# Attention, two mixture-of-experts layers on one core: VectorE divides the second half of x before it sums the next tile's squares

## The chip, the cores and the metric

The kernel runs on one core of a Trainium2 chip. The metric is the device time of one execution in microseconds (us). Five engines work side by side, each through its own list of instructions in order, and wait for each other by semaphores: PE (TensorE, matrix products), DVE (VectorE), ACT (ScalarE), POOL (GpSimd) and SP (SyncE, which here issues most transfers).

## The reference

Three stages follow each other: attention by random features for 4 batches, 8 heads, 576 positions and 64 dimensions; a mixture of 4 experts in which every expert runs on every token; and a second mixture in which 32 slots gather from all tokens. Only the first stage is touched by the change:

```
def phi(x):                                   # x is q or k, scaled
    proj = np.einsum('bhsd,md->bhsm', x, omega)
    sq = np.sum(x * x, axis=-1, keepdims=True) / 2.0
    h = proj - sq
    h = h - np.max(h, axis=-1, keepdims=True)
    return np.exp(h) / np.sqrt(m)
q_p, k_p = (phi(q_s), phi(k_s))
kv = np.einsum('bhsm,bhsd->bhmd', k_p, v)
z = np.sum(k_p, axis=2)
num = np.einsum('bhsm,bhmd->bhsd', q_p, kv)
den = np.einsum('bhsm,bhm->bhs', q_p, z)[..., None] + 1e-06
return (num / den).astype(np.float32)
```

The result, 2304 tokens of 512 features (`x` below), feeds the first mixture: `h = np.maximum(x @ w1[e], 0.0); out += p[:, e:e + 1] * (h @ w2[e])`.

## The kernel before, in words

The 2304 tokens are 18 tiles of 128. Attention goes through 36 steps, one tile of keys ("k") or of queries ("q") a step. Five k-tiles come first; from step 5 on q and k alternate, up to step 30 (the last k); steps 31 to 35 are q. So the even steps from 6 to 30 are k-steps.

In a step the tiles of several steps are at work at once. What is issued, and in which order on every engine, is a line of two-letter names in the table `orders` (line 310): "k" for a k-step, "q" for a q-step, "qq" for a q behind a q, "" for the drain. `work` (line 321) gives each name its function and its lag: a name with lag 3 works in step i on tile i-3. An engine takes its instructions in the order of these names. No scheduler moves them afterwards.

- `P0`, `P1` (`project`, lines 195 to 197): PE multiplies a tile's first and second four heads with omega into the PSUM tile `pj`, one of three banks in turn.
- `M0`, `M1` (`maximum`, L203), `a0`, `a1` (`bias1`, L208), `b0`, `b1` (`bias2`, L213): DVE's reductions that make the bias `nb` of the exponentials. `a` reads the maximum and the tile's sum of squares.
- `E0`, `E1` (`exps`, L220): ACT makes the features `fe`, four heads in four instructions.
- `S` (`split`, lag -3, L167 on ACT, or on DVE for the last tiles; L170 to L172 on POOL): ACT rounds the tile's numbers into `hi`; POOL computes the rest `lo` (L170), the squares (L171) and a first fold of them (L172).
- `Q` (`squares`, lag -1): DVE sums the next tile's squares (L186), and L187 scales them into the tile `stat`.
- `K0`, `K1` (`accumulate`, L239): PE adds a k-tile's features times v to `kv`.
- `T0`, `T1` (`turn`, lag 1, L253): PE transposes a q-tile's features, ACT copies them (L254).
- `N0`, `N1` (`attend`, lag 3, L263): PE multiplies a q-tile's features with `kv` into `num`, both halves through one PSUM bank.
- `D0`, `D1` (`divide`, lag 3): DVE divides the first and second half (L273, L274, L275) into `x`.
- `X` (`store_x`, lag 4, L284) and `R` (`store_rest`, L290): PE transposes x, ACT and DVE split it for the next stage.

In a k-step `D1` divides the q-tile of three steps before; the q-step behind it transposes that tile's x in `X`. `D1` has work in the k-steps 8 to 30, twelve in all.

Of the kernel before, what the change touches and what calls it, by code (L numbers as in the profile page):

```python
# [17 lines left out]
B, H, S, D = 4, 8, 576, 64  # L18
# [31 lines left out]
def body(ctx: ExitStack, tc: tile.TileContext, ql, kl, vl, om, dp, wl, phi, w2l, out):  # L50
# [244 lines left out]
    def to_dram():  # L295
# [12 lines left out]


    orders = {  # L310
# [1073 lines left out]
```

## Time and profile before

| | |
|---|---|
| time, median of 3 runs | 938.43 us (935.58 to 938.77) |
| profiled execution | 936.1 us, of which the span of the trace is 934.3 us |
| busy share of the span | PE 99%, DVE 80%, ACT 45%, POOL 38% |
| attention stage | the first 150 us of the span, about |
| one k-step and the q-step behind it | 7.70 us |

The span runs from the first to the last instruction of the one profiled execution; the busy shares are means over all stages. The 1.8 us between the profiled time and its span lie outside the trace. PE's share, near 100%, says that it is seldom without work, not that each product runs at its best rate.

### The profile page before, as it was taken

The numbers are of one execution on the slowest core, as the hardware profiler recorded it, in microseconds if no ns is written. First come the engines' busy times: TensorE is split into PE (matmuls) and PEld (weight loads), VectorE is DVE, ScalarE is ACT, GpSimd is POOL, SyncE is SP. The second block draws the span as 40 slices with busy tenths as digits, with TensorE's granted clock in tenths as the row PEclk, the third lists the DMA queues.
The fourth block names the chain that finished last, engine by engine and source line by source line (L and its number), as shares of the span: only waits on it lengthen the run. The fifth ranks groups of instructions, "written<-read, shape, count | busy, mean of one in ns | idle before, by whom it ended". The sixth has DMA issues, their size and how long they took to land.

```text
span 934.3 us, 15959 instructions
## 1 busy us (share of the span) xinstructions
PE 922.3 (99%) x6132; PEld 889.4 (95%) x6132; DVE 750.5 (80%) x1142; ACT 419.7 (45%) x833; POOL 353.4 (38%) x298
## 2 busy tenths in 40 slices
PE   8999999999999999999999999999999999999997
PEld 8999999999999999999999999999999999999734
DVE  7888897999899888888878878887888888878433
ACT  5899875425543434334243333432433434223423
POOL 7978872422443341434053423423241434000100
PEclk9999999999999999999999999999999999999999
DMA  7778768685869675887767666767666776867997
GB/s 259 233 249 299 245 212 267 212 306 175 318 207 343 225 250 197 303 263 264 243 215 254 209 230 214 245 207 258 200 240 203 249 239 201 301 213 276 384 408 309
DMA packets 80510, 236.51 MB, mean 253 GB/s; under 512 B 6636, under 2 KB 34612, under 8 KB 78388
## 3 DMA queue, kind: packets, MB, share of 16 engines
q1 hardware_dynamic: 76260, 222.82, 69.5%
q10 hardware_dynamic: 3744, 9.67, 2.6%
q0 software_dynamic: 432, 3.01, 0.8%
q8 instruction: 48, 0.79, 0.3%
q14 instruction: 26, 0.21, 0.1%
HBM read 211.86 MB, written 23.63 MB: 252 GB/s over the span
## 4 chain that ended last, share of the span: by engine, by line
PE 88%; DVE 7%; ACT 2%; issue 1%; DMA 1%; SPq 0%; POOL 0%; ACTq 0%; DVEq 0%
PE X L809 19%; PE X L633 19%; PE B L633 15%; PE B L809 15%; PE kv L239 3%; PE num L263 3%; PE pj L195 2%; PE so L1233 2%; PE tp L253 2%; PE hq L1205 2%; PE pj L196 2%; PE pj L197 1%; DVE x L831 1%; DMA raw<-kl 1%; PE tpx L284 1%
## 5 line engine op out<-in xcount | busy, mean ns | idle before, releaser
L441 POOL TENSOR_TENSOR Tw<-raww 128x512 f32<-128x512 f32 x30 | 39.8, 1349 | 200.8 <-DMA raww<-wl 200.8
L831 DVE TENSOR_TENSOR x<-X,x 128x768 f32<-128x768 f32 x84 | 79.9, 951 | 40.1 <-PE X L809 39.9
L633 PE MATMUL X<-x,w1h 128*128 128x384 f32 x432 | 110.0, 335 | 0.0
L633 PE MATMUL B<-x,w1h 128*128 128x384 f32 x432 | 109.9, 335 | 0.0
L633 PE MATMUL X<-x,w1x 128*128 128x384 f32 x504 | 94.2, 334 | 0.0
L633 PEld LDWEIGHTS X<-x,w1x 128*128 128x128 f32 x504 | 87.9, 188 | 0.3 <-issue 0.3
L220 ACT ACTIVATE fe<-pj,nb 128x128 f32<-128x128 f32 x288 | 82.8, 390 | 10.1 <-DVE nb L213 9.4
L680 ACT CAST s3h<-X 128x768 fp32r<-128x768 f32 x21 | 16.8, 802 | 143.9 <-DVE X L690 143.9
L633 PEld LDWEIGHTS X<-x,w1h 128*128 128x128 f32 x432 | 77.8, 188 | 0.2 <-ACT u L704 0.2
L633 PEld LDWEIGHTS B<-x,w1h 128*128 128x128 f32 x432 | 77.8, 188 | 0.0
L831 DVE TENSOR_TENSOR x<-B,x 128x768 f32<-128x768 f32 x72 | 68.3, 948 | 6.0 <-PE B L809 5.5
L633 PE MATMUL X<-x,w1l 128*128 128x384 f32 x216 | 72.3, 335 | 0.1
L633 PE MATMUL B<-x,w1l 128*128 128x384 f32 x216 | 72.2, 334 | 0.0
L460 POOL TENSOR_TENSOR w2l<-raww,w2h 128x512 fp32r<-128x512 f32 x24 | 36.4, 1530 | 73.4 <-ACT w2h L459 73.4
L704 ACT COPY u<-X 128x768 f32<-128x768 f32 x63 | 50.0, 794 | 23.0 <-PE X L633 23.0
L460 POOL TENSOR_TENSOR w2l<-Tw,w2h 128x512 fp32r<-128x512 f32 x32 | 47.4, 1492 | 26.6 <-ACT w2h L459 26.6
L203 DVE TENSOR_REDUCE stat<-pj 128x4 f32<-128x512 f32 x72 | 49.3, 685 | 7.1 <-PE pj L197 6.5
L170 POOL TENSOR_TENSOR lo<-raw,hi 128x512 fp32r<-128x512 f32 x35 | 44.7, 1278 | 19.0 <-ACT hi L167 14.5
L680 ACT CAST e11h<-B 128x768 fp32r<-128x768 f32 x21 | 16.8, 801 | 77.4 <-PE B L809 68.5
L460 POOL TENSOR_TENSOR w1l<-raww,w1h 128x512 fp32r<-128x512 f32 x25 | 37.6, 1506 | 33.6 <-ACT w1h L459 33.5
L460 POOL TENSOR_TENSOR w1x<-Tw,w1x 128x512 fp32r<-128x512 f32 x21 | 27.5, 1312 | 58.4 <-ACT w1x L459 58.4
L680 ACT CAST e12h<-s 128x768 fp32r<-128x768 f32 x24 | 20.1, 836 | 61.5 <-DVE s L620 61.5
(268 smaller groups left out, 2763.4 us busy)
## 6 DMA issues: line engine op xcount, KB each, us to landing
x<-xt SPq DMA_DIRECT2D x84, 768.0 KB, 4.8
x<-xd SPq DMA_DIRECT2D x75, 768.0 KB, 4.6
raww<-wl SPq DMA_DIRECT2D x16, 1024.0 KB, 6.8
raw<-ql SPq DMA_DIRECT2D x18, 512.0 KB, 5.1
xd<-xst SPq DMA_DIRECT2D x36, 256.0 KB, 3.1
prb<-prd SPq DMA_DIRECT2D x23, 384.0 KB, 6.6
raw<-kl SPq DMA_DIRECT2D x16, 512.0 KB, 5.8
w2tb<-w2l SPq DMA_DIRECT2D x6, 1024.0 KB, 6.8
```

Source lines behind the costliest of these rows:

```text
L170: (nc.gpsimd if i else nc.vector).tensor_tensor(out=lo, in0=r, in1=f32(hi), op=ALU.subtract)
L203: nc.vector.tensor_reduce(out=stats(i)[:, 4 * g:4 * g + 4, 0], in_=pjs[i, g], axis=AX.X, op=ALU.max)
L220: nc.scalar.activation(out=feats[i][:, 4 * g + h, :], in_=pjs[i, g][:, h, :], func=AF.Exp, bias=biases[i, g][:, h:h + 1], scale=1.0,)
L239: nc.tensor.matmul(kvps[b][h // 4][:, h % 4, :], lhsT=feats[i][p0:p0 + np_, h, :], rhs=v[p0:p0 + np_, h, :], start=first and h % 4 == 0, s ...
L263: nc.tensor.matmul(num[p0:p0 + n, h, :], lhsT=fts[i][:, 4 * g + h, p0:p0 + n], rhs=kvt[b][:, 4 * g + h, :], start=True, stop=True,)
L441: nc.gpsimd.tensor_tensor(out=out_, in0=a, in1=b_, op=op)
L460: nc.gpsimd.tensor_tensor(out=lo, in0=src, in1=f32(hi), op=ALU.subtract)
L633: nc.tensor.matmul(o, lhsT=lhs[:, jp, c], rhs=rhs[:, :, k, :], start=first and not k and not n, stop=False, skip_group_check=True,)
L680: nc.scalar.copy(out=pair(hs[i][0]), in_=src)
L704: nc.scalar.copy(out=pair(tmp({I1: "u1", I6: "u2", I5: "u4"}[i])), in_=q)
L809: nc.tensor.matmul(q[:, c, :], lhsT=lhs[:, jp, cs], rhs=rhs[:, jp, :], start=i in (I1, I2, I7) and jp == 0 and m == 0, stop=False, skip_gr ...
L831: nc.vector.tensor_tensor(out=o, in0=q, in1=o, op=ALU.add)
```

## The change

In the line "k" of the table, `D1` moves ahead of `Q`. Nothing is added or removed; every other line of the table stays.

```
--- before.py
+++ after.py
@@ -308,7 +308,7 @@
 
 
     orders = {
-        "k": "P0 N0 M0 D0 T0 P1 a0 K0 b0 M1 a1 E0 K1 T1 N1 S b1 Q D1 E1 X R",
+        "k": "P0 N0 M0 D0 T0 P1 a0 K0 b0 M1 a1 E0 K1 T1 N1 S b1 D1 Q E1 X R",
         "q": "P0 P1 N0 D0 M0 K1 N1 a0 X S M1 b0 Q a1 D1 T0 R E0 K0 b1 E1 T1",
         "qq": "P0 N0 M0 X D0 P1 N1 M1 a0 Q b0 R a1 T0 E0 D1 b1 K0 K1 S T1 E1",
         "": "W X N0 D0 R N1 T0 D1 W T1",
```

It reorders DVE's list in twelve places, and no other engine's. The first rows show one of the twelve, DVE in a k-step between the bias of the second half (L213, `b1`) and the maxima of the q-step behind it (L203, `M0`); "waits" names the semaphores that an instruction waits for.

```order
 L208 TENSOR_REDUCE stat<-stat 128x4 [waits DVE_49]
 L213 TENSOR_REDUCE nb<-stat 128x4 [waits DVE_49]
+L273 TENSOR_SCALAR rd<-num 128x4 [waits PE_49]
+L274 RECIPROCAL rd<-rd 128x4 [waits DVE_49]
+L275 TENSOR_TENSOR x<-num,rd 128x256 [waits DVE_49]
 L186 TENSOR_REDUCE sq<-raw 128x8 [waits DMAHW1_49,Pool_49]
 L187 TENSOR_SCALAR stat<-sq 128x8 [waits DVE_49]
-L273 TENSOR_SCALAR rd<-num 128x4 [waits PE_49]
-L274 RECIPROCAL rd<-rd 128x4 [waits DVE_49]
-L275 TENSOR_TENSOR x<-num,rd 128x256 [waits DVE_49]
 L203 TENSOR_REDUCE stat<-pj 128x4 [waits PE_49]
 L208 TENSOR_REDUCE stat<-stat 128x4 [waits DVE_49]
```

The three instructions of the division, of which the first waits for PE, now stand ahead of the two of the sums of squares.

The second rows are DVE in step 30, the last k-step, where L167 (the rounding of `split`) is DVE's too.

```order
 L167 CAST hi<-raw 128x512 [waits DMAHW0_49]
 L213 TENSOR_REDUCE nb<-stat 128x4 [waits DVE_49]
+L273 TENSOR_SCALAR rd<-num 128x4 [waits PE_49]
+L274 RECIPROCAL rd<-rd 128x4 [waits DVE_49]
+L275 TENSOR_TENSOR x<-num,rd 128x256 [waits DVE_49]
 L186 TENSOR_REDUCE sq<-raw 128x8 [waits DMAHW4_49,Pool_49]
 L187 TENSOR_SCALAR stat<-sq 128x8 [waits DVE_49]
-L273 TENSOR_SCALAR rd<-num 128x4 [waits PE_49]
-L274 RECIPROCAL rd<-rd 128x4 [waits DVE_49]
-L275 TENSOR_TENSOR x<-num,rd 128x256 [waits DVE_49]
 L203 TENSOR_REDUCE stat<-pj 128x4 [waits PE_49]
 L208 TENSOR_REDUCE stat<-stat 128x4 [waits DVE_49]
```

The same five instructions change places here: L187 now stands directly ahead of the next step's L203.

## Rows read from the trace of the kernel before

**Rows 1.** The page: span, and part 1 (busy time, share of the span, instructions)

```profile
span 934.3 us, 15959 instructions
...
PE 922.3 (99%) x6132; PEld 889.4 (95%) x6132; DVE 750.5 (80%) x1142; ACT 419.7 (45%) x833; POOL 353.4 (38%) x298
```

**Rows 2.** Windows: one pair of steps, 43.94 to 51.64 us; the first line names the columns

```profile
core 0: us, PE busy (x) PEld busy (x) DVE busy (x) ACT busy (x) POOL busy (x), PEclk, DMA share, GB/s
...
43.94:51.64 7.70, 7.70 (x71) 7.70 (x69) 6.73 (x24) 7.01 (x22) 5.97 (x7) 1.00 0.78 242
```

**Rows 3.** Waits of PE in the attention stage, 0 to 165 us

```profile
PE pj L195 <- ACT fe L220: 1.1, 2, 0.7
...
PE tpx L284 <- DVE x L275: 0.6, 1, 0.6
```

**Rows 4.** Timeline of DVE, steps 10 and 11: start, length, work [idle before <-releaser]

```profile
45.72 0.16 DVE L213 TENSOR_REDUCE nb<-stat 128x4 f32<-128x8 f32 x1
...
46.86 0.16 DVE L213 TENSOR_REDUCE nb<-stat 128x4 f32<-128x8 f32 x1
46.94 0.42 DVE L186 TENSOR_REDUCE sq<-raw 128x8 f32<-128x256 f32 x1
47.39 0.17 DVE L187 TENSOR_SCALAR stat<-sq 128x8 f32<-128x8 f32 x1
47.47 0.15 DVE L273 TENSOR_SCALAR rd<-num 128x4 f32<-128x4 f32 x1
...
48.21 0.68 DVE L203 TENSOR_REDUCE stat<-pj 128x4 f32<-128x512 f32 x1
...
49.60 0.15 DVE L213 TENSOR_REDUCE nb<-stat 128x4 f32<-128x8 f32 x1
...
50.12 0.38 DVE L187 TENSOR_SCALAR stat<-sq 128x8 f32<-128x8 f32 x1
50.40 0.15 DVE L208 TENSOR_REDUCE stat<-stat 128x4 f32<-128x8 f32 x1
...
51.08 0.14 DVE L213 TENSOR_REDUCE nb<-stat 128x4 f32<-128x8 f32 x1
51.64 0.69 DVE L203 TENSOR_REDUCE stat<-pj 128x4 f32<-128x512 f32 x1 [0.42 <-PE pj L197]
```

**Rows 5.** Timeline of POOL, the same steps

```profile
48.19 1.28 POOL L170 TENSOR_TENSOR lo<-raw,hi 128x512 fp32r<-128x512 f32 x1 [1.58 <-ACT hi L167]
49.43 1.03 POOL L171 TENSOR_TENSOR raw<-raw 128x512 f32<-128x512 f32 x1
...
51.22 1.28 POOL L170 TENSOR_TENSOR lo<-raw,hi 128x512 fp32r<-128x512 f32 x1
```

**Rows 6.** Timeline of PE, the same steps and the next

```profile
46.17 1.00 PE L263 MATMUL num<-kvt,ft 128*128 128x65 f32 x8
...
51.33 0.28 PE L197 MATMUL pj<-om_hi,lo 128*128 128x256 f32 x1
...
52.28 0.61 PE L253 MATMUL tp<-ident,fe 128*128 128x128 f32 x4
...
53.44 0.60 PE L253 MATMUL tp<-ident,fe 128*128 128x128 f32 x4
```

**Rows 7.** Timeline of ACT, the same steps

```profile
45.97 1.14 ACT L220 ACTIVATE fe<-pj,nb 128x128 f32<-128x128 f32 x4 [0.17 <-DVE nb L213]
...
50.14 2.25 ACT L220 ACTIVATE fe<-pj,nb 128x128 f32<-128x128 f32 x8
```

**Rows 8.** Timeline of DVE: line 187 in steps 8, 25 and 30

```profile
39.78 0.17 DVE L187 TENSOR_SCALAR stat<-sq 128x8 f32<-128x8 f32 x1
...
106.02 0.17 DVE L187 TENSOR_SCALAR stat<-sq 128x8 f32<-128x8 f32 x1
...
126.88 1.03 DVE L187 TENSOR_SCALAR stat<-sq 128x8 f32<-128x8 f32 x1
```

**Rows 9.** Timeline of POOL beside the last two

```profile
106.05 0.73 POOL L172 TENSOR_TENSOR raw<-raw 128x256 f32<-128x256 f32 x1
...
126.58 1.29 POOL L170 TENSOR_TENSOR lo<-raw,hi 128x512 fp32r<-128x512 f32 x1 [0.58 <-PE num L263]
```

**Rows 10.** Timeline of PE in step 31

```profile
128.69 0.44 PE L284 MATMUL tpx<-ident,x 128*128 128x128 f32 x2 [0.60 <-DVE x L275]
```

2 rows, old and new, of the table orders are left out of this document.

## The prediction

> **What bounds the kernel now.** I read the page first: PE is busy for 99% of the span [rows 1], so time is lost or won only where PE waits or gets less to do. The windows come next. A k-step and the q-step behind it take 7.70 us, and in them PE is busy for all 7.70, ACT for 7.01, DVE for 6.73 and POOL for 5.97, with PE's clock granted in full [rows 2]. So the attention stage is PE's, but DVE and ACT have under a microsecond to spare per pair. The waits say how little can be won: over the attention stage PE waits 0.6 us, once, for an x from the division, and 1.1 us for the exponentials [rows 3]. A change of DVE's order can therefore gain about a microsecond of 936, and lose more if it makes DVE late by more than the slack that PE's operands have. The timeline of one pair shows that slack; I use steps 10 and 11, which repeat nearly to 0.01 us in the pairs around them.
>
> **What the change moves.** In twelve k-steps the same five DVE instructions run in another order. Their sum would not change if each took as long as before. Two things speak against that.
>
> First, the division waits for PE's second product. In step 10 the bias L213 stands at 46.86 and the next instruction starts 0.08 later, at 46.94 [rows 4]. The product N1 runs from 46.17 to 47.17 [rows 6], and DVE starts 0.03 after PE's end (L197 ends at 51.61 [rows 6], DVE's L203 starts at 51.64 [rows 4]). So L273 can start at 47.20, not at 46.94: DVE idles 0.26 us, which L186 and L187 filled before.
>
> Second, L187 is short only where POOL leaves it alone. It takes 0.17 us in steps 8, 10 and 25, but 0.38 in step 11 and 1.03 in step 30 [rows 4, 8]. In step 11 POOL's L171 runs from 49.43 to 50.46 and L187 ends at 50.50; in step 30 POOL's L170 runs from 126.58 to 127.87 and L187 ends at 127.91 [rows 4, 5, 8, 9]. So an L187 that starts inside a POOL instruction ends 0.04 us after it. One that starts first goes through: in step 25 it starts at 106.02, 0.03 ahead of POOL's L172, and takes 0.17 [rows 8, 9].
>
> The Trainium skill, page "SBUF — State Buffer", section "SBUF: two separate sides", says that VectorE in a mode with two ports and GpSimd hold a port pair exclusively for a whole instruction, and that whoever starts first makes the other wait. These rows agree that the first one wins. Read literally, a blocked L187 would run its own 0.17 us after POOL's end, 0.13 more than the 0.04 that the rows show; with two collisions in each of the five costly pairs (below) that would make the sum 5.3 us instead of 4.0. I go by the rows.
>
> Now the walk through steps 10 and 11 as changed. From the division's first instruction to whatever follows it takes 0.74 us (47.47 to 48.21), and from L186 to L187 0.45 (46.94 to 47.39) [rows 4]. So L273 is at 47.20, L186 at 47.94, L187 at 48.39. POOL's L170 runs from 48.19 to 49.47 [rows 5]; it is released by ACT, which the moved instructions do not touch here. L187 starts 0.20 us inside it and ends at 49.51. An instruction behind a long L187 starts 0.10 before its end (50.12 + 0.38 = 50.50, next at 50.40 [rows 4]), so M0 of step 11 starts at 49.41 instead of 48.21: **1.20 us late**.
>
> In step 11, L187 came 1.91 us after M0 [rows 4], so it is now at 51.32. POOL's next L170 starts at 51.22 and runs to 52.50 [rows 5]: blocked again, this time for longer than the 0.38 of before. It ends at 52.54, the next L208 starts at 52.44 instead of 50.40, and b1, 0.68 later, at 53.12 instead of 51.08: **2.04 us late**.
>
> Who waits for that? The exponentials E1 of step 11, then PE's T1 of step 12. ACT starts 0.09 after the bias's end (45.72 + 0.16, then 45.97) and four exponentials take 1.14 [rows 4, 7]: from 53.35 to 54.49, where all eight of the step were done at 52.39 before [rows 7]. T1 starts at 53.44 [rows 6], and N1 behind it one period after 46.17, at 53.87. Four transposes in 0.43 us, one for each head, put the last at 53.76; now it can start at 54.49 + 0.03. PE loses **0.76 us**, and since it has no idle time to give back, the end of the program moves by as much. The other consumers stand in slack: the sums of squares are read a step later, x is ready earlier than before, and E0 of step 11, for which b0 is 1.20 us late (49.60, now 50.80 [rows 4]), runs from 51.05 to 52.19, just ahead of its reader T0 at 52.28 [rows 6].
>
> In the next pair (steps 12 and 13) DVE is late enough (M0 at 53.19, 1.55 late, against 0.76 for PE) that the division no longer waits for N1. Then the race on POOL goes the other way. Counted from b0's start, L187 comes at (46.86 - 45.72) + 0.08 + 0.74 + 0.45 = 2.41 us; the exponentials E0 start 0.25 after it (45.97) and L170 2.22 after those (48.19), so at 2.47 [rows 4, 5, 7]. ACT's copies between E0 and L170 follow DVE now, so L187 is 0.06 us first and takes 0.17. In that pair's q-step it meets the POOL instruction that it met before and takes about 0.4. DVE uses its idle 0.42 us [rows 4] and the wait ahead of D0, and is back on PE's pace at the end. So I expect costly and free pairs in turn.
>
> The sum over the twelve: steps 8, 12, 16, 20 or 10, 14, 18 and so on, four costly pairs of the seven from 8 to 20, 4 x 0.76 = 3.0 us. The three pairs at 22, 24 and 26 have additional POOL work and L187s that are held up already; I give them anything from 0 to 0.76 each and take 0.8 together. Step 28 is costly again, 0.8, but step 30 gives back: there D1 stood behind the L187 of 1.03 us, and PE waited 0.60 us for x [rows 8, 10]. With D1 ahead of it that wait goes: 0.8 - 0.6 = 0.2. Together 3.0 + 0.8 + 0.2 = **4.0 us**, 936.1 to 940.1 for the profiled execution. That execution lies 2.3 us below the median of the three runs, so on the median's scale it is 942.4. I say 942.
>
> **The rivals.**
>
> *Every pair is costly* (slower). The lead of 0.06 us in the second pair is about what a single gap varies by. If POOL comes first there too, DVE carries (49.51 - 48.39 - 0.17) + (52.54 - 51.32 - 0.38) = 0.95 + 0.84 = 1.79 us more per pair, against some 0.6 of waiting that it can give up (the 0.42 and a part of the wait for D0); pairs then grow by between 0.76 and 1.2 us. For eleven pairs that is 8 to 13, less step 30's 0.6: a median of 946 to 951. For it: the margin is thin. Against it: neighbouring pairs repeat to 0.01 us, so a lead of 0.06 can be a lasting one.
>
> *The q-step's collision does not happen* (no change). In step 11 L187 comes only 0.10 us behind the start of L170. If my gaps are 0.1 too long, it passes first, b1 is 1.2 us late instead of 2.04, and 2.04 cost only 0.76, so lateness under 1.28 costs nothing. The pairs then cost 0, step 30 gives back up to 0.6, and the time is 935.5 to 936.5 on the profile's scale, 938 to 939 on the median's. The decision lies with 0.1 us in step 11.
>
> *Faster.* If L187 slipped past POOL in the k-steps too, only the earlier x would remain. PE's waits for the division are 0.6 us in total [rows 3], so the gain is at most that, far below what can be measured.
>
> **How the numbers follow.** Costly and free pairs in turn, 940 to 944: 0.50. Every pair costly, 945 to 951: 0.24. No collision in the q-step, or another slack that I did not see, 937 to 940: 0.23. A gain: 0.03. Runs of this kernel differ by 0.3%, and I take 0.5%, 4.7 us, as the least that can be told from no change, so the border is 943.1. Of the likeliest case a third lies above it: slower 0.24 + 0.16 = 0.40, faster 0.03 (only by the spread of runs), the rest 0.57 the same. The range of 8 in 10 reaches from 937.5, the free case, to 949, inside the rival of every pair; the likeliest case's own is 940 to 944.
>
> **What would show it.** Right: L187 in the k-steps 8, 12, 16, 20 at about 1.1 us and ending 0.04 after POOL's L170, and 0.17 in the steps between; an idle 0.26 us ahead of L273 that names PE's product; in the q-steps behind, L187 at 1.2; PE waiting some 0.8 us for L220 ahead of T1 every second pair; the tpx wait of 0.60 gone or smaller; pairs of 7.70 us and about 8.46 us in turn. Wrong: L187 at 0.17 in all k-steps (POOL gave way), or at 1.1 in all of them with every pair above 8.4 us, or PE without waits although DVE is late by 2 us, which would mean that T1 has more slack than the rows give.

## The result and the profile after

| | before | after | ratio, 95% interval |
|---|---|---|---|
| median of 5 runs | 937.31 us | 943.54 us (942.36 to 945.47) | 1.0069 (1.0058 to 1.0081) |
| the changed kernel once more, 5 runs, beside 27 of before | 936.60 us | 941.04 us (940.53 to 942.52) | 1.0050 (1.0038 to 1.0063) |

The kernel became slower, by 4.4 to 6.2 us. The page of the changed kernel, span and part 1, against [rows 1]:

```profile
span 941.5 us, 15959 instructions
...
PE 926.6 (98%) x6132; PEld 889.6 (94%) x6132; DVE 758.0 (81%) x1142; ACT 419.9 (45%) x833; POOL 354.0 (38%) x298
```

The span is 7.2 us longer with the same number of instructions. DVE is busy for 7.5 us more and PE for 4.3 us more, though neither has more to do: their instructions last longer. L187, all its 36 runs before and then in the changed kernel (shortest, median and longest in ns; added up 14.3 and 24.4 us):

```profile
L187 DVE TENSOR_SCALAR stat<-sq x36: 174/326/1055, 8.3 to 142.2; 128x8 f32<-128x8 f32 x36
```

```profile
L187 DVE TENSOR_SCALAR stat<-sq x36: 174/605/1232, 8.5 to 148.0; 128x8 f32<-128x8 f32 x36
```

The timeline of DVE in steps 8, 9 and 10 (start, length, work), where [rows 4] showed the same places one pair later:

```profile
40.39 0.16 DVE L213 TENSOR_REDUCE nb<-stat 128x4 f32<-128x8 f32 x1
40.67 0.16 DVE L273 TENSOR_SCALAR rd<-num 128x4 f32<-128x4 f32 x1
...
41.42 0.41 DVE L186 TENSOR_REDUCE sq<-raw 128x8 f32<-128x256 f32 x1
41.87 1.09 DVE L187 TENSOR_SCALAR stat<-sq 128x8 f32<-128x8 f32 x1
42.87 0.68 DVE L203 TENSOR_REDUCE stat<-pj 128x4 f32<-128x512 f32 x1
...
44.32 0.41 DVE L186 TENSOR_REDUCE sq<-raw 128x8 f32<-128x256 f32 x1
44.77 1.23 DVE L187 TENSOR_SCALAR stat<-sq 128x8 f32<-128x8 f32 x1
45.90 0.15 DVE L208 TENSOR_REDUCE stat<-stat 128x4 f32<-128x8 f32 x1
...
46.57 0.14 DVE L213 TENSOR_REDUCE nb<-stat 128x4 f32<-128x8 f32 x1
46.64 0.67 DVE L203 TENSOR_REDUCE stat<-pj 128x4 f32<-128x512 f32 x1
...
50.50 0.17 DVE L187 TENSOR_SCALAR stat<-sq 128x8 f32<-128x8 f32 x1
50.58 0.68 DVE L203 TENSOR_REDUCE stat<-pj 128x4 f32<-128x512 f32 x1
```

POOL beside it:

```profile
41.65 1.28 POOL L170 TENSOR_TENSOR lo<-raw,hi 128x512 fp32r<-128x512 f32 x1 [0.86 <-ACT hi L167]
42.88 1.04 POOL L171 TENSOR_TENSOR raw<-raw 128x512 f32<-128x512 f32 x1
...
44.69 1.27 POOL L170 TENSOR_TENSOR lo<-raw,hi 128x512 fp32r<-128x512 f32 x1
...
50.62 1.27 POOL L170 TENSOR_TENSOR lo<-raw,hi 128x512 fp32r<-128x512 f32 x1 [2.86 <-ACT hi L167]
```

PE's product N1 of step 8:

```profile
39.63 1.00 PE L263 MATMUL num<-kvt,ft 128*128 128x65 f32 x8
```

In step 8 the bias L213 starts at 40.39 and the division at 40.67, 0.04 behind the end of N1 (40.63), so the wait for it is there. L187 starts at 41.87, 0.22 us inside POOL's L170, and ends at 42.96, 0.03 behind it. In step 9 it starts at 44.77, 0.08 inside the next L170, and lasts 1.23. In step 10 it starts at 50.50, 0.12 ahead of L170, and takes 0.17. From step 8 on, L187 in the k-steps takes 1.09, 0.17, 1.09, 0.17, 1.17, 0.17, 1.08, 0.17, 0.47, 0.18, 1.09 and 0.29 us, where before it was 0.17 to 0.19 in ten of the twelve.

ACT and PE at the end of the first costly pair (E1 of step 9, then T1 and N1 of step 10):

```profile
46.75 1.14 ACT L220 ACTIVATE fe<-pj,nb 128x128 f32<-128x128 f32 x4 [1.17 <-DVE nb L213]
```

```profile
47.17 1.10 PE L253 MATMUL tp<-ident,fe 128*128 128x128 f32 x4
48.19 1.08 PE L263 MATMUL num<-kvt,ft 128*128 128x65 f32 x8
```

ACT stood idle 1.17 us for the bias ahead of these exponentials. The four transposes of T1, 0.60 us in [rows 6], are spread over 1.10, and N1 starts 1.02 us behind them instead of 0.43. So the loss does not stand in the list of PE's waits: it is in the length of a group whose first transposes could run.

Where it accrues can be read from the starts of M0 (L203) in the k-steps:

| M0 of step | 8 | 10 | 12 | 16 | 20 | 24 | 28 | first product of the next stage |
|---|---|---|---|---|---|---|---|---|
| before, us | 36.24 | 43.94 | 51.64 | 67.04 | 82.26 | 98.01 | 115.45 | 146.63 |
| after, us | 37.39 | 46.64 | 53.73 | 70.05 | 86.17 | 103.03 | 120.82 | 152.73 |
| difference | 1.15 | 2.70 | 2.09 | 3.01 | 3.91 | 5.02 | 5.37 | 6.10 |

The first 1.15 us lie ahead of any moved instruction (the 256 KB loads of the first tiles landed after a median of 5.4 us in this execution and of 4.2 before). From step 8 to the next stage the change costs 6.10 - 1.15 = **4.95 us**: 0.94, 0.92, 0.90 and 1.11 for each two pairs up to step 24, 0.35 for the next two, and 0.73 for the last. The remaining 7.2 - 6.10 = 1.1 us lie behind the attention stage.

### The profile page after: what moved, and what is told of

It is laid out like the page before. It is cut to its first block, busy times and chain, and to the rows that moved or that the text cites. A ratio compares the mean times of both kernels' runs of the same rounds, so it can differ in the third digit from the quotient of the medians.

```text
span 941.5 us, 15959 instructions
## 1 busy us (share of the span) xinstructions
PE 926.6 (98%) x6132; PEld 889.6 (94%) x6132; DVE 758.0 (81%) x1142; ACT 419.9 (45%) x833; POOL 354.0 (38%) x298
## 3 DMA queue, kind: packets, MB, share of 16 engines
q0 software_dynamic: 432, 3.01, 0.8%
## 4 chain that ended last, share of the span: by engine, by line
PE 84%; DVE 10%; ACT 2%; issue 2%; DMA 1%; SPq 0%; POOL 0%; ACTq 0%; DVEq 0%
PE X L809 19%; PE X L633 19%; PE B L633 15%; PE B L809 14%; PE kv L239 3%; PE num L263 2%; PE tp L253 2%; PE so L1233 2%; PE hq L1205 2%; PE pj L195 1%; DVE x L831 1%; PE pj L196 1%; PE pj L197 1%; DVE stat L187 1%; DVE stat L203 1%
## 5 line engine op out<-in xcount | busy, mean ns | idle before, releaser
L220 ACT ACTIVATE fe<-pj,nb 128x128 f32<-128x128 f32 x288 | 83.8, 394 | 19.5 <-DVE nb L213 18.1
L170 POOL TENSOR_TENSOR lo<-raw,hi 128x512 fp32r<-128x512 f32 x35 | 44.7, 1278 | 24.3 <-ACT hi L167 18.9
L203 DVE TENSOR_REDUCE stat<-pj 128x4 f32<-128x512 f32 x72 | 49.2, 684 | 3.2 <-PE pj L197 2.3
L195 PE MATMUL pj<-om_hi,hi 128*128 128x256 f32 x144 | 45.4, 315 | 2.5 <-ACT hi L167 1.3
```

The costliest lines, as they stand in the source:

```text
L170: (nc.gpsimd if i else nc.vector).tensor_tensor(out=lo, in0=r, in1=f32(hi), op=ALU.subtract)
L195: nc.tensor.matmul(o, lhsT=hi[:, pi, :], rhs=om_hi, start=True, stop=False)
L203: nc.vector.tensor_reduce(out=stats(i)[:, 4 * g:4 * g + 4, 0], in_=pjs[i, g], axis=AX.X, op=ALU.max)
L220: nc.scalar.activation(out=feats[i][:, 4 * g + h, :], in_=pjs[i, g][:, h, :], func=AF.Exp, bias=biases[i, g][:, h:h + 1], scale=1.0,)
```

## The experiments

The theory: L187, moved behind the division, starts inside a POOL instruction and is held until its end; two such collisions in a pair make DVE later than PE's operands allow. The rivals: the order itself costs (DVE idles ahead of L273, and the sums come late), or the collision of the k-step alone is the loss. Unless an experiment says otherwise it computes what the kernel computes. Times are medians; every ratio is to the kernel before on the same chip, 936.9 us beside the first four and 936.6 beside the others.

**The collision without the change.** Two idle instructions behind D1, in the order of before:

```diff
+    def extra(i, g):
+        junk = pa.tile([P, H], F32, name="junk", tag="junk")
+        nc.vector.tensor_reduce(out=junk, in_=stats(i + 1)[:, :, 1:2], axis=AX.X, op=ALU.add)
+        nc.vector.tensor_scalar_mul(junk, junk, -c)
...
-        "k": "P0 N0 M0 D0 T0 P1 a0 K0 b0 M1 a1 E0 K1 T1 N1 S b1 Q D1 E1 X R",
+        "k": "P0 N0 M0 D0 T0 P1 a0 K0 b0 M1 a1 E0 K1 T1 N1 S b1 Q D1 Z E1 X R",
```

> The order of before, with two idle instructions put behind D1 in the twelve k-steps on DVE: a small reduction and then a scaling of 128x8 numbers of the same kind as L187. They compute nothing that is used. Theory (L187 behind the division is held up by POOL's L170, and the lateness of DVE reaches PE through E1 and T1): the scaling starts about 0.2 us after L170 and lasts about 1.1 us, in the second pair of two as well because it stands 0.2 us later than L187 does in the changed kernel; the time is 5 to 13 us above before. Rival (the order itself costs, because DVE idles for PE's product ahead of L273 and the sums come late): nothing is moved here, so the time is at most 1 us above before, and the scaling lasts 0.17 us.

Measured: 949.75 us, ratio 1.0137 (1.0122 to 1.0152), 12.9 us above before. The idle instructions over all twelve k-steps (L281, L282), then step 10 on DVE and on POOL:

```profile
L281 DVE TENSOR_REDUCE junk<-stat x12: 154/156/158, 40.9 to 141.3; 128x8 f32<-128x8 f32 x12
L282 DVE TENSOR_SCALAR junk<-junk x12: 172/1224/1239, 41.1 to 141.5; 128x8 f32<-128x8 f32 x12
```

```profile
48.81 0.17 DVE L187 TENSOR_SCALAR stat<-sq 128x8 f32<-128x8 f32 x1
48.89 0.15 DVE L273 TENSOR_SCALAR rd<-num 128x4 f32<-128x4 f32 x1
...
49.63 0.16 DVE L281 TENSOR_REDUCE junk<-stat 128x8 f32<-128x8 f32 x1
49.82 1.23 DVE L282 TENSOR_SCALAR junk<-junk 128x8 f32<-128x8 f32 x1
50.96 0.68 DVE L203 TENSOR_REDUCE stat<-pj 128x4 f32<-128x512 f32 x1
```

```profile
49.75 1.27 POOL L170 TENSOR_TENSOR lo<-raw,hi 128x512 fp32r<-128x512 f32 x1 [2.86 <-ACT hi L167]
```

The scaling starts 0.07 us behind L170 and lasts 1.23; in eleven of the twelve k-steps it is held up, in both of two neighbouring pairs, and a pair takes 8.98 us (M0 at 45.76, 54.74, 63.71) instead of 7.70. Nothing was moved, and DVE's list got 12 instructions of 0.16 us and 12 that take 0.17 where POOL lets them pass.

**The same without a scaling.** The second idle instruction is a reduction:

```diff
-        nc.vector.tensor_scalar_mul(junk, junk, -c)
+        nc.vector.tensor_reduce(out=junk, in_=junk.unsqueeze(2), axis=AX.X, op=ALU.add)
```

> The same as the run with the scaling behind D1, but the second idle instruction is a reduction of 128x8 numbers instead of a scaling. Theory (POOL holds up the scaling and not reductions): each of the two lasts about 0.16 us, DVE is some 0.3 us late per k-step, within its slack, and the time is that of before within 1 us. Rival (any more work or lateness on DVE at this place costs PE): the time is 2 us or more above before, near that of the run with the scaling.

Measured: 937.74 us, ratio 1.0011 (1.0002 to 1.0019). The idle instructions, then step 10 on DVE and on POOL:

```profile
L281 DVE TENSOR_REDUCE junk<-stat x12: 153/156/158, 41.1 to 129.1; 128x8 f32<-128x8 f32 x12
L282 DVE TENSOR_REDUCE junk<-junk x12: 160/161/164, 41.3 to 129.3; 128x8 f32<-128x8 f32 x12
```

```profile
48.89 0.16 DVE L282 TENSOR_REDUCE junk<-junk 128x8 f32<-128x8 f32 x1
```

```profile
48.67 1.27 POOL L170 TENSOR_TENSOR lo<-raw,hi 128x512 fp32r<-128x512 f32 x1 [1.53 <-ACT hi L167]
```

A reduction of the same 128x8 numbers at the same place never lasts longer than 0.164 us, though all 24 idle ones start inside a POOL instruction (here 0.22 us inside L170). So it is the scaling that POOL holds up, and not the place or the added work that costs 12 us.

**The change without L187 on DVE.** ACT scales, in all steps:

```diff
     def squares(i):
...
-        nc.vector.tensor_scalar_mul(stat[:, :, 1], sq, -c)
+        sqs[i] = sq
...
+    def scale(i):
+        nc.scalar.activation(out=stats(i)[:, :, 1], in_=sqs[i], func=AF.Copy, scale=-c)
...
-        "k": "... S b1 D1 Q E1 X R",
+        "k": "... S b1 D1 Q L E1 X R",
```

`L` is `scale`, the scaling by itself; `Q` keeps the sum.

> The changed order, but the scaling of L187 is done by ACT (ahead of E1 in k-steps, ahead of E0 in q-steps), in all 36 steps. DVE keeps L186. Theory (the collision of L187 with POOL is the loss): nothing of DVE's list waits for POOL any more, the idle 0.26 us ahead of L273 stays, and the time falls back to before's, between 3 us below it and 1 us above. Rival (the idle time ahead of L273 is the loss, the collision is only seen): the time stays 4 to 7 us above before, as in the changed kernel. A risk to both: ACT has 0.7 us to spare per pair and gets about 0.4 more, so a microsecond or two may be lost on ACT.

Measured: 937.06 us, ratio 1.0009 (0.9995 to 1.0023). DVE's waits from 36 to 135 us (L277 is the division's first instruction here):

```profile
DVE stat L207 <- PE pj L201: 7.4, 13, 1.0
...
DVE rd L277 <- PE num L267: 4.0, 10, 2.3
```

DVE waits for PE's product ahead of the division in ten places, 4.0 us in total. The longest, 2.3, is that of step 24, which waits with the order of before too (1.7 us in the kernel before, 1.9 in the next run); the other nine wait 0.19 us each. The time is that of before. The idle time ahead of the moved division costs nothing that can be measured: the rival that blames the order falls.

**The order of before with the same move to ACT** (the same edit, with "... S b1 Q L D1 E1 X R").

> The order of before with the same move of the scaling from DVE to ACT. Theory: within 1 us of the run with the changed order and ACT's scaling, since without L187 the place of D1 does not matter; against before 0 to 3 us faster, since the long L187s of before (1.03 us in step 30, 0.4 in most q-steps) are gone too. Rival (the order itself costs): 4 to 7 us faster than the changed order with ACT's scaling.

Measured: 936.85 us, ratio 1.0003 (0.9991 to 1.0015), within 0.2 us of the run above. Without L187 on DVE the place of D1 does not matter. The hoped gain over before does not show in the time. In the two traces the stretch from the first division to the first product of the next stage takes 108.90 and 108.82 us, 0.65 and 0.73 less than the 109.55 of before, and PE's wait of 0.60 us for x is gone in both; apart from that one the long L187s of before lay in DVE's slack.

**ACT scales in the q-steps alone**, so that only the k-step's collision is left in the changed order:

```diff
+    def scale(i):
+        if seq[i - 1][0] == "k":
+            nc.vector.tensor_scalar_mul(stats(i)[:, :, 1], sqs[i], -c)
+        else:
+            nc.scalar.activation(out=stats(i)[:, :, 1], in_=sqs[i], func=AF.Copy, scale=-c)
```

> The changed order; ACT does the scaling of L187 in the q-steps alone, DVE keeps it in the k-steps, behind the division. Theory (the k-step's collision makes DVE 1.2 us late, which E1 and T1 still have slack for; it takes the q-step's collision on top, 2.04 us, to reach PE): L187 still lasts about 1.1 us in every second k-step or so, and the time is within 1.5 us of before. Rival (the collision in the k-step alone is the loss, the q-step's only follows): 4 to 7 us above before, as in the changed kernel.

Measured: 937.02 us, ratio 1.0003 (0.9994 to 1.0012). DVE's scalings in the k-steps (L192 here):

```profile
L192 DVE TENSOR_SCALAR stat<-sq x18: 174/558/1171, 11.1 to 129.3; 128x8 f32<-128x8 f32 x18
```

They still last 1.08 to 1.17 us in five of the twelve moved places (1.08 in step 8, 0.17 in step 10, 1.09 in step 12, and so on). So it takes the collisions of the k- and of the q-step together to cost what the changed kernel loses. The k-step's alone is not quite free: from the first division to the M0 of step 24 this trace takes 61.75 us, 0.82 more than before (60.93), where the changed kernel takes 64.80, 3.87 more. In the time it does not show: at the next stage 0.30 us of it are left (109.85 against 109.55), and PE's wait of 0.60 us for x is gone here too.

**Half of the change**: L186 ahead of the division, L187 behind it.

```diff
-        "k": "... S b1 D1 Q E1 X R",
+        "k": "... S b1 Q D1 L E1 X R",
```

> Half of the change: L186 stays ahead of the division, L187 alone goes behind it in the k-steps. By the walk, L187 comes at 48.13 in step 10, 0.06 us ahead of POOL's L170 at 48.19. Theory (whoever starts first goes through, even by so little): L187 takes 0.17 us in the k-steps and the time is that of before within 1 us. Rival (a start so close counts as a collision, or L187's place behind the division costs by itself): L187 lasts about 1.1 us and the time is 5 us or more above before.

Measured: 937.13 us, ratio 1.0006 (0.9997 to 1.0014). L187 (L191 here) and POOL in step 10:

```profile
48.25 0.16 DVE L191 TENSOR_SCALAR stat<-sq 128x8 f32<-128x8 f32 x1
```

```profile
48.42 1.28 POOL L170 TENSOR_TENSOR lo<-raw,hi 128x512 fp32r<-128x512 f32 x1 [1.57 <-ACT hi L167]
```

It starts 0.17 us ahead of POOL and passes, as in all seven k-steps from 8 to 20; the smallest lead is 0.04 us, in step 16. In steps 22 and 24, where POOL has additional work, it lasts 1.13 and 0.92, and 1.23 in step 25; the M0 of step 28 is 0.31 us late by it, and the time does not show it. The expected 0.17 did not hold there; the expected time did.

**POOL later instead of DVE earlier**: in the changed order, S behind E1 in the k-steps.

```diff
-        "k": "... K1 T1 N1 S b1 D1 Q E1 X R",
+        "k": "... K1 T1 N1 b1 D1 Q E1 S X R",
```

> The changed order, and in k-steps S (the rounding of split on ACT and POOL's L170 to L172 behind it) is put behind E1, so that POOL's L170 starts about 1 us later, near 49.2 in step 10. Everything that DVE does stands as in the changed kernel. Theory (the place of L187 against POOL decides, not its place on DVE): L187 of the k-step, due at 48.39, takes 0.17 us, and the time falls back to before's within 1.5 us. Rival (DVE's order is the loss): 4 to 7 us above before.

Measured: 937.66 us, ratio 1.0011 (1.0002 to 1.0020). Step 10 on DVE and POOL:

```profile
48.73 0.18 DVE L187 TENSOR_SCALAR stat<-sq 128x8 f32<-128x8 f32 x1
```

```profile
49.53 1.27 POOL L170 TENSOR_TENSOR lo<-raw,hi 128x512 fp32r<-128x512 f32 x1 [1.56 <-ACT hi L167]
```

L187 has the same place on DVE as in the changed kernel and takes 0.18; in eleven of the twelve moved places it is at most 0.20. Of the 4.4 us that the changed kernel loses on this chip 3.4 are gone, by a later start of POOL's work. Counted from the first division, M0 is where it was before to within 0.04 us up to step 28 (78.33 us, and 78.37 before). The 1.0 us by which the stretch to the next stage is still longer (110.54) comes in behind that; what causes it is not shown.

**The changed kernel again.**

> The changed kernel again, for a second profile. The first one lost 4.95 us between the first division (37.08 before, 38.23 after) and the first product of the next stage (146.63, 152.73); the rest of its 7.2 us lay ahead of the first division (1.15) and behind (1.1). Theory (only the attention stage is touched): again 4.8 to 5.1 us in the attention stage and L187 long and short in the same turn; the parts ahead and behind differ from the first profile's. Rival (the next stage is slower too): again about a microsecond behind the attention stage.

Measured: 941.04 us, as in the table above. L187 in the second profile:

```profile
L187 DVE TENSOR_SCALAR stat<-sq x36: 174/602/1236, 8.9 to 147.6; 128x8 f32<-128x8 f32 x36
```

Its times in the k-steps come in the same turn (1.09, 0.17, 1.08, 0.17, 1.17, 0.17, 1.08, 0.17, 0.47, 0.17, 1.08, 0.28). From the first division (37.78) to the first product of the next stage (152.30) are 114.52 us, against 114.50 in the first profile and 109.55 before: **4.97 us** again. Behind that product lie 788.4 us, against 788.8 and 787.7; in the other kernels' profiles it is 787.2 to 789.2, so the rest of the first difference is the scatter of one execution.

## Why the prediction was right

The forecast was 942.0 us in a range of 937.5 to 949, from a loss of 4.0 us; measured were 943.5 and 941.0. That the time itself comes so close is in part luck. The forecast stood on a median of 938.4 from three runs; the later medians of before are 1.1 and 1.8 us lower (937.3 and 936.6), which makes up for much of a loss that was forecast too small, 3.6 us above that median against 6.2 and 4.4. Why the two measured losses differ by 1.8 us is not shown; by the two traces it is not the attention stage, which lost 4.95 and 4.97. Against the prediction's own border of 0.5% the first measurement is slower and the second lies on it.

- *The bound and what can be won.* Right. PE stayed the engine that sets the time; the earlier x gave back 0.36 us of PE's wait and no more.
- *The division waits 0.26 us for PE.* Right, a little smaller: in step 8 it starts 0.28 behind the bias instead of 0.08, so it idles 0.20, and by the run with ACT's scaling this costs nothing itself. In step 10, where no wait was expected, there are 0.09 left: the bias is at 49.14 and the division at 49.31, 0.04 behind the end of N1.
- *L187 collides with POOL's L170 in the k-step and again in the q-step, M0 1.20 and b1 2.04 us late.* Right: L187 lasts 1.09 and 1.23 us, where the walk gave 1.12 and 1.22. M0 of step 9 starts at 42.87, where before's 40.60 and the 1.15 by which this execution is later from the start give 41.75, so it is 1.12 late. And b1 of step 9 starts at 46.57, where before's 43.38 and the 1.15 give 44.53, so it is 2.04 late. That both are needed was left to the rival without the q-step's collision; the run with ACT in the q-steps shows it, at the time of before and 0.8 us against 3.9 in the trace.
- *T1 pays, 0.76 us for each costly pair.* The right place, 0.2 us too small: 0.94, 0.92 and 0.90 measured for a costly and a free pair together. I let N1 follow the last transpose at the usual 0.11 us. N1 was at 46.17 before and at 48.19 after, of which 1.15 is the earlier difference of the two executions, so it lost 0.87. From there to the N1 of step 12 (55.97) it takes 7.78 us instead of 7.70: the free pair costs 0.08, where it stood at nothing. What holds N1 back for the 0.1 us beyond the walk, and what the 0.08 are, is not shown.
- *Costly and free pairs in turn.* Right for all of steps 8 to 22. The lead that lets L187 through is 0.12 us in step 10, not 0.06, and it sufficed in both profiles. The rival "every pair is costly" did not come, but the run with the idle scaling shows about its price: 1.28 us a pair, 12.9 in all, where I gave 8 to 13.
- *Steps 22 to 26 at 0.8, steps 28 and 30 at 0.2 together.* The sum up to the M0 of step 24 was 3.87 where 4 x 0.76 and a share of the 0.8 stood, from there to step 28 0.35, and the last part cost 0.73. That the L187s of 22 to 26 were held up already held for the first of these pairs alone (0.49 and 0.92 us before); in steps 24 to 26 they took 0.17 to 0.19. Step 30 gave back less than hoped: PE's wait for x is still there, 0.24 of the 0.60 us of [rows 10]:

```profile
141.68 0.44 PE L284 MATMUL tpx<-ident,x 128*128 128x128 f32 x2 [0.24 <-DVE x L275]
```

- *The sum.* 4.0 forecast, 4.95 and 4.97 measured between the first division and the next stage. The term mis-sized most is the price of a costly pair with the free one behind it, 0.76 for about 0.92: four of them make 3.7 instead of 3.0. Steps 22 to 26 then took about 0.5 instead of 0.8, and what lies behind them 0.7 instead of 0.2. Of these last 0.5, 0.24 are missing from step 30's gift (0.36 for 0.6); the rest stays open.
- *Signs.* I looked for PE's wait in the list of waits; it stood in the stretched T1, and only the idle time of ACT ahead of L220 names it. The pairs in turn came: from N1 to N1 they take 8.56 and 7.78 us, where 8.46 and 7.70 were expected. From M0 to M0, on DVE, it is 9.25 and 7.09.

No version beat the kernel before: six of the experiments equal it within 0.2%.

## What to carry to other kernels

A small scaling between two SBUF tiles on DVE can last as long as the POOL instruction that it meets, so its place is to be chosen against POOL's timeline, and not only against its operands and readers. Before an instruction is moved, look whether the lengths of its runs are spread (0.17 to 1.06 us here for one shape): the spread says that it waits inside itself for something, and where the long ones end says for what. Lateness on an engine that is not the bound costs little until it passes the slack of the bound engine's operands: over steps 8 to 24 one collision of 1.1 us in every second pair cost 0.8 us in all, two in a row 3.9.

## What the runs showed of the hardware that was not expected

- A held L187 runs nearly all its own time inside the wait: it ended 0.02 to 0.04 us behind POOL's end, not 0.17. The Trainium skill, page "SBUF — State Buffer", section "SBUF: two separate sides", says that the one that starts second fully blocks. The trace agrees on who wins and on a wait to the end of the winner's instruction; what the loser still takes after that is measured here. No run here shows whether L187 runs in the mode with two ports of which that section speaks.
- DVE gets in between two POOL instructions that follow each other without a gap: by the records of step 8, L170 ends at 42.93, L171 starts at 42.88, and L187 ends at 42.96 all the same.
- The races of L187 against L170 in steps 8, 9 and 10, with margins of 0.08 to 0.22 us, were decided the same way in each of two executions: the twelve lengths of L187 in the k-steps agree to 0.01 us. A start 0.06 to 0.10 us too late (the idle scaling, nine times) made it last 1.02 to 1.07 us longer.
- Twelve scalings of 128x8 numbers cost 12.0 us more than twelve reductions of the same size at the same place (949.75 and 937.74).
